# Attention and two mixture layers on one core: the first mixture layer's work behind the attention, 256 or 512 tokens at a time

## The chip, the core and the metric

The kernel runs on one core of a Trainium2 chip. The core has TensorE (PE, matrix products into the banks of PSUM), VectorE (DVE), ScalarE (ACT), GpSimd (POOL) and SyncE (SP, whose queue issues all transfers here); each takes its own instructions strictly in order and waits on semaphores for the others. The metric is the device time of one execution in microseconds, the median of several runs.

## What is computed

Causal attention with a cumulative decay over 4 x 8 heads of 576 tokens and 64 dimensions, and then two feed-forward ("mixture") layers over 2304 tokens of 512 numbers. Cut to what matters:

```python
x = attention(q, k, v, f)                  # (2304, 512)
h = x @ w_in                               # (2304, 2048)
r = np.maximum(h, 0.0)
g = s * (r * r) + b
x = g @ w_out                              # (2304, 512): first mixture layer
h = x @ w2_in                              # (2304, 1024): second mixture layer
solu = h * softmax(h)
out = layernorm(solu, g_ln) @ w2_out       # (2304, 512)
```

## The kernel before, in words

Every product is made of parts. An operand is split into hi (rounded to the type fp32r) and lo (what is left), and a product is the sum of hi x hi, hi x lo and lo x hi, three products on PE.

**Order of the work.** The function declares pieces (`add`, line 72) with the names of what they read and write, an estimated duration and a priority. `Plan.run` (line 96) plays them through by these estimates: PE takes the ready piece with the lowest priority number, every other engine the one with the lowest sum of ready time and priority. The instructions are issued in that order, so each engine's queue, SP's too, is fixed when the kernel is built. Transfers with a negative priority go at once; others wait in the plan while more than 3 us of transfers are outstanding.

**Stages.** Attention comes first (some 316 us). The first mixture layer has two passes, because its weights don't all fit beside the attention: the first pass applies three of the eight slices of 256 hidden units (`first`) to all tokens and stores the sum to `x2p_d`; the second applies the other five (`rest`) and adds that sum. Then comes the second layer, 18 tiles of 128 tokens (`tile2`, line 883).

**One chunk of the first layer** (`job`, line 787) is 256 tokens. `x_load` (line 760) fetches x in two summands from `xs_d` (one into `xraw`, one into `xlo`), adds them, and splits the sum into `xhi` and `xlo`; both passes do this. For each slice there are 24 products of h (lines 807 to 818, 128 x 128 weights against 256 columns), the gate (relu on ACT, line 822; the square, line 823; gh, line 844 to 846; gl, line 833), and 24 products of x2 (lines 852 to 864). PE's priority is 4 per slice for h and 4 per slice + 9 for x2, so that h of the next two slices comes ahead of x2 of a slice, and 100 per chunk:

```python
add("PE", 6 * mm(CH), h_mm, ..., 1000 + 100 * n + 4 * m)
add("PE", 6 * mm(CH), x_mm, ..., 1000 + 100 * n + 4 * m + 9)
```

Then x2 is emptied into `x2o` and stored (first pass by ACT, line 871; second pass by DVE with `x2p`, line 868).

**What is there twice.** The first four chunks (`NB`) run among the attention's pieces with one bank for h and two for x2. When the attention is over, `extend` (line 1017) opens tiles in its place: a second pair `xhi1`, `xlo1`, a second x2 of two banks and three more banks for h. From chunk 4 on, jobs alternate between the two pairs of x buffers (`j = n % 2`) and of x2, and rotate over four banks of h. Chunk 4 itself uses the old pair and the old x2, which don't depend on `extend` (the name `"ext"`). r is there twice, gh and gl three times.

**Beside this stage** the second pass's weights and the second layer's are loaded and unpacked from 64-bit floats (`load_w`, line 696: transfer, ACT line 713, DVE lines 715, 717 and 720, then hi and lo), from the end of the attention on.

Of the kernel before, what the change touches and what calls it, by code (L numbers as in the profile page):

```python
# [20 lines left out]
FS = (3, 3, 3, 3, 3, 3, 3, 3, 3)  # L21
# [39 lines left out]
class Plan:  # L61
    """Orders the work of all engines: of the pieces whose inputs are there by an estimate, each engine takes the first.

    Pieces are declared in an order that is right; which of them have to wait for which follows from the names of what
    they read and write. The instructions are then issued in the order in which the pieces start by the estimate."""
# [6 lines left out]
    def add(self, eng, dur, fn, r=(), w=(), pri=0, bytes=None, after=(), until=None):  # L72
        """An engine's piece of dur ns, or by engine a choice of (dur, fn); bytes for a transfer; lower pri first."""
# [22 lines left out]
    def run(self):  # L96
# [87 lines left out]
def mm(n):  # L184
    return 2 + n / 2.4
# [3 lines left out]
def kernel(  # L189
# [38 lines left out]
    x2_d = dram.tile([KD, 128, NT], F32, name="x2_d")  # L228

# [12 lines left out]
    ident = const.tile([128, 128], F32, name="ident")  # L242
    mask = const.tile([128, 512], F32, name="mask")
    maskt = const.tile([128, 288], F32, name="maskt")
# [16 lines left out]
    xhis, xlos = ([moe.tile([128, KD, CH], F32R, name=x)] for x in ("xhi", "xlo"))  # L261
# [3 lines left out]
    QW = S + 64  # L265
    raw = tiles(att, [128, 2, S], F32, "raw", 2)
# [22 lines left out]
    # The first batch's first blocks have the mixture layer's banks as well.  # L289
# [62 lines left out]
    # Two pairs side by side. Their scores come by products of their parts, and their decay by products with rows of ones.  # L352
# [17 lines left out]
    # The tensor engine's clock rises after some microseconds of work on all rows: products of zeros until the first ones.  # L370
# [44 lines left out]
    def early_split(g):  # L415
        """The parts of two pairs' queries and keys."""
# [9 lines left out]
    # The odd heads' queries have their last rows first.  # L426
# [4 lines left out]
    def take(keys):  # L431
        """The tiles of these names pass from one use to the next."""
# [5 lines left out]
    # Both heads' first two blocks of queries, one head's third and fourth, both heads' tails, the other head's third  # L438
    # and fourth. The first batch's first blocks come first, for the mixture layer to start with them.
# [60 lines left out]
    def unit(s, p, i):  # L500
# [3 lines left out]
        if part:  # L504
# [5 lines left out]
            def scores(x, c, kc):  # L510
                """The products that make 128 queries' scores."""
# [100 lines left out]
        if tl:  # L612
            # The last 64 keys of the tails; lo goes below hi.
# [146 lines left out]
    def x_load(n, c, src, hi, lo, khi, klo, b=BX, x=[]):  # L760
        """Loads tokens and splits them; from the attention they come in two parts."""
# [5 lines left out]
        for g in range(2 if first else 1):  # L767
# [5 lines left out]
            if src is xs_d:  # L773
# [4 lines left out]
                add("SP", 650, lambda lo_=lo_, view=view: nc.sync.dma_start(out=f32(lo_()), in_=view[1]), rk + x, kl,  # L778
                    min(b, BS), bytes=512 * sz)
                P.first = P.first or len(P.ops) - 1  # L780
                tt(lambda raw_=raw_: raw_, lambda raw_=raw_: raw_, lambda lo_=lo_: f32(lo_()), sz, ALU.add, kl, kx, b)
            else:
                dma(raw_, src[ks, :, cs].rearrange("k p t -> p k t"), [("x2d", c)], kx, 512 * sz, b)
            copy(hi_, lambda raw_=raw_: raw_, sz, kx + x, kh, b)
            tt(lo_, lambda raw_=raw_: raw_, lambda hi_=hi_: f32(hi_()), sz, ALU.subtract, kx + kh, kl, b)

    def job(n, c, fps, last, b=BMOE):
        ext = n >= NB
        j = n % 2 if ext else 0
        khi, klo = (("xx", 2), ("xx", 3)) if j == 0 else (("xhi1",), ("xlo1",))  # L790
        hi, lo = (lambda: xhis[j]), (lambda: xlos[j])
        x_load(n, c, xs_d, hi, lo, khi, klo, x=["ext"] if j else [])
        nh = 4 if ext else 1
        jx2 = n % 2 if ext else 0
        kx2 = ("x2", jx2)
        x2 = lambda: x2ps[jx2]
        if last:
            dma_late(lambda: late["x2p"], x2p_d[:, :, c * CH:(c + 1) * CH].rearrange("k p t -> p k t"),
                     [("x2pd", c)], ["x2p"], 524288)
        for m, fp in enumerate(fps):  # L800
            ta, tb, ka, kb = weights[fp]
            jh = slot("h4", 4) if ext else 0
            kh = ("h", jh)
            h = lambda jh=jh: hps[jh]
            for g in range(2):
                for u in range(2):
                    def h_mm(u=u, g=g, h=h, ta=ta):
                        wh, wl = ta[0], ta[1]
                        for kc in (2 * g, 2 * g + 1):
                            o = kc * 256 + u * 128  # L810
                            a_, b_ = wh[:, o:o + 128], wl[:, o:o + 128]
                            t = h()[:, u, :]
                            for x, (w_, v_) in enumerate(((a_, hi()), (a_, lo()), (b_, hi()))):
                                nc.tensor.matmul(t, w_, v_[:, kc, :], start=kc == 0 and u == 0 and x == 0,  # L814
                                                 stop=kc == KD - 1 and x == 2, skip_group_check=True)

                    add("PE", 6 * mm(CH), h_mm, [khi + (g,), klo + (g,)] + wkeys(ka) + (["ext"] if jh else []), [kh],
                        1000 + 100 * n + 4 * m)
            jr, jg = slot("r", 2), slot("g", 3)
            r, gh, gl = rs_[jr], ghs[jg], gls[jg]  # L820
            kr, kgh, kgl = ("r", jr), ("gh", jg), ("gl", jg)
            add("ACT", act_p(512), lambda h=h, r=r: nc.scalar.activation(out=r, in_=h(), func=AF.Relu), [kh], [kr], b)  # L822
            def square(eng, r=r):
                if eng == "DVE":
                    nc.vector.scalar_tensor_tensor(out=r, in0=r, scalar=s_sb, in1=r, op0=ALU.mult, op1=ALU.mult)
# [287 lines left out]
```

## Time and profile before

| what | value |
|---|---|
| median of 3 runs | 901.32 us |
| lowest and highest | 900.86 and 901.57 us |
| span of the profiled execution | 902.3 us |
| own time of that execution | its span; none besides it is recorded |
| PE busy | 840.7 us, 93% |
| DVE, ACT, POOL busy | 538.8, 445.5, 355.7 us |
| products on PE | 5749, with as many weight loads |

The span is the time between the first and the last instruction of one execution, on the only core. Times in rows count from the span's start. A line number is that of the kernel before; L316 to L325 are helpers that copy, or add and subtract two tensors. "gl<-r,b_sb,gh" reads: gl is written from r, b_sb and gh. PE's products are pipelined, so the length of a single one (some 280 ns) is more than the distance to the next one's start. A wait's "releaser" is the instruction that ended it.

### The profile page before, as it was taken

What the parts mean: (1) busy time and instruction counts of PE and PEld (TensorE: products, weight loads), DVE (VectorE), ACT (ScalarE), POOL (GpSimd) and SP (SyncE); (2) the same over time, 40 slices, a digit from 0 to 9 for tenths busy, and PEclk for the clock granted to TensorE, in tenths of its full rate; (3) what the DMA queues carried; (4) which work ended last, traced back from release to release, by engine and by line L of the source; (5) the groups of instructions that cost most, each with busy time, mean ns of one, the idle gap of its engine ahead of it and who ended that gap; (6) DMA issues with size and microseconds to landing.
All of it is one profiled execution on the core that took longest, in us unless ns stands there. A gap on an engine that the chain in (4) does not pass through costs nothing.

```text
span 902.3 us, 15528 instructions
## 1 busy us (share of the span) xinstructions
PE 840.7 (93%) x5749; PEld 782.7 (87%) x5749; DVE 538.8 (60%) x1122; ACT 445.5 (49%) x981; POOL 355.7 (39%) x398
## 2 busy tenths in 40 slices
PE   7868889889899999898989999999999999999998
PEld 7747778888899999797989999999998888888886
DVE  8888897768678747877988321222213544444451
ACT  4666678758688646554355324332332333333342
POOL 6768786645645355545634111111113401111000
PEclk7689799999899999999999999999999999999999
DMA  6689999799896275664455312232112111100001
GB/s 197 163 206 235 247 258 248 183 251 226 201 232 189 86 271 176 194 198 135 141 187 187 95 45 73 71 94 86 32 47 71 48 46 48 46 24 12 24 36 46
DMA packets 84413, 120.82 MB, mean 134 GB/s; under 512 B 7010, under 2 KB 62818, under 8 KB 84338
## 3 DMA queue, kind: packets, MB, share of 16 engines
q1 hardware_dynamic: 84338, 119.84, 48.0%
q8 instruction: 45, 0.74, 0.3%
q14 instruction: 30, 0.25, 0.1%
HBM read 70.12 MB, written 23.89 MB: 104 GB/s over the span
## 4 chain that ended last, share of the span: by engine, by line
PE 60%; DMA 14%; DVE 12%; issue 5%; ACT 4%; POOL 3%; SPq 2%; ACTq 0%; POOLq 0%; DVEq 0%
PE h L814 13%; PE ph L916 10%; PE x L860 5%; PE x L861 5%; PE x L858 5%; PE po L960 4%; PE po L959 4%; PE po L961 4%; DMA k<-raw 3%; PE S L549 2%; DVE wr L717 2%; PE PT L601 2%; DVE wr L720 2%; PE O L670 2%; DMA k<-Hh 2%
## 5 line engine op out<-in xcount | busy, mean ns | idle before, releaser
L835 DVE SCALAR_TENSOR_TENSOR gl<-r,b_sb,gh 128x512 fp32r<-128x512 f32 x65 | 55.9, 860 | 134.3 <-POOL gh L846 132.9
L814 PE MATMUL h<-xhi,u 128*128 128x256 f32 x720 | 134.0, 283 | 0.0
L846 POOL TENSOR_SCALAR gh<-r,b_sb 128x512 fp32r<-128x512 f32 x57 | 46.3, 812 | 197.0 <-ACT r L828 169.1
L586 POOL TENSOR_SCALAR e<-e,m 128x128 f32<-128x128 f32 (+4 forms) x144 | 101.0, 713 | 53.7 <-DVE m L582 32.8
L814 PEld LDWEIGHTS h<-xhi,u 128*128 128x128 f32 x720 | 114.3, 192 | 0.0
L822 ACT ACTIVATE r<-h 128x512 f32<-128x512 f32 x72 | 42.8, 594 | 131.2 <-PE h L814 127.7
L858 PE MATMUL x<-gh,u 128*128 128x256 f32 x360 | 103.3, 287 | 3.9 <-POOL gh L846 3.9
L860 PE MATMUL x<-gl,u 128*128 128x256 f32 x360 | 103.9, 288 | 1.6 <-DVE gl L835 1.4
L861 PE MATMUL x<-gh,u 128*128 128x256 f32 x360 | 103.2, 287 | 0.0
L814 PE MATMUL h<-xlo,u 128*128 128x256 f32 x360 | 102.0, 283 | 0.0
L573 ACT ACTIVATE e<-e,m 128x128 f32<-128x128 f32 (+4 forms) x144 | 84.0, 586 | 19.8 <-DVE m L536 19.3
L814 PE MATMUL h<-xhi,w 128*128 128x256 f32 x432 | 86.5, 287 | 2.0 <-POOL xhi L316 2.0
L601 PE MATMUL PT<-ident,e 128*128 128x128 f32 x384 | 65.1, 296 | 15.3 <-DVE pbl L609 8.5
L549 PE MATMUL S<-k,q 68*128 68x384 f32 (+2 forms) x248 | 65.5, 375 | 9.8 <-DMA k<-raw 3.4
L858 PEld LDWEIGHTS x<-gh,u 128*128 128x128 f32 x360 | 70.5, 196 | 4.3 <-POOL gh L846 4.3
L814 PEld LDWEIGHTS h<-xhi,w 128*128 128x128 f32 x432 | 71.1, 193 | 2.8 <-POOL xhi L316 2.3
L536 DVE CUSTOM_DVE_ANT_0 e<-S,mask 128x512 f32<-128x512 f32 (+4 forms) x136 | 63.1, 486 | 16.6 <-PE S L549 13.8
L860 PEld LDWEIGHTS x<-gl,u 128*128 128x128 f32 x360 | 70.4, 196 | 2.4 <-DVE gl L835 2.4
L860 PE MATMUL x<-gl,w 128*128 128x256 f32 x216 | 63.8, 295 | 7.7 <-DVE gl L835 5.2
L861 PEld LDWEIGHTS x<-gh,u 128*128 128x128 f32 x360 | 70.6, 196 | 0.0
L814 PEld LDWEIGHTS h<-xlo,u 128*128 128x128 f32 x360 | 69.2, 192 | 0.0
L916 PE MATMUL ph<-w,xh 128*128 128x512 f32 x256 | 68.7, 390 | 0.0
(214 smaller groups left out, 2224.3 us busy)
## 6 DMA issues: line engine op xcount, KB each, us to landing
xraw<-xs_d SPq DMA_DIRECT2D x17, 512.0 KB, 4.5
xlo<-xs_d SPq DMA_DIRECT2D x17, 512.0 KB, 4.7
q<-Hh SPq DMA_DIRECT2D x28, 288.0 KB, 5.8
k<-Hh SPq DMA_DIRECT2D x28, 288.0 KB, 7.7
wraw<-in_moe_w_in_dram SPq DMA_DIRECT2D x14, 512.0 KB, 3.8
wraw<-in_moe_w_out_dram SPq DMA_DIRECT2D x14, 512.0 KB, 4.5
xs_d<-xt SPq DMA_DIRECT2D x16, 320.0 KB, 4.3
raw<-in_moe_w_in_dram SPq DMA_DIRECT2D x10, 512.0 KB
```

The source lines that it names most:

```text
L536: nc.vector.tensor_tensor_reduce(out=e_, in0=sp, in1=mk, scale=-scale, scalar=init, op0=ALU.add, op1=ALU.min, accum_out=acc)
L549: nc.tensor.matmul(o, a, b, start=i == 0, stop=i == len(mms) - 1)
L573: nc.scalar.activation(out=e[:, c], in_=e[:, c], func=AF.Exp, scale=-1.0, bias=m[:, j:j + 1], accum_out=m[:, 2 + j:3 + j])
L586: nc.gpsimd.tensor_scalar(out=e[:, c], in0=e[:, c], scalar1=m[:, 4 + j:5 + j], scalar2=1.0, op0=ALU.mult, op1=ALU.mult)
L601: nc.tensor.transpose(pt[:, kb, :], e[:, 128 * kb:128 * kb + 128], ident)
L814: nc.tensor.matmul(t, w_, v_[:, kc, :], start=kc == 0 and u == 0 and x == 0, stop=kc == KD - 1 and x == 2, skip_group_check=True)
L835: nc.vector.scalar_tensor_tensor(out=gl, in0=r, scalar=b_sb, in1=f32(gh), op0=ALU.add, op1=ALU.subtract)
L846: "POOL": (662, lambda r=r, gh=gh: nc.gpsimd.tensor_scalar(out=gh, in0=r, scalar1=1.0, scalar2=b_sb, op0=ALU.mult, op1=ALU.add))}, 0, 0, [ ...
L858: nc.tensor.matmul(t, a_, gh[:, u, :], start=st and u == 0 and d % 2 == 0, stop=False, skip_group_check=True)
L860: nc.tensor.matmul(t, a_, gl[:, u, :], start=False, stop=False, skip_group_check=True)
L861: nc.tensor.matmul(t, b_, gh[:, u, :], start=False, stop=fin and u == 1, skip_group_check=True)
L916: nc.tensor.matmul(h()[:, n:n + 512], st_, mv[:, n:n + 512], start=kc == 0 and mv is wh and st_ is a, stop=kc == KD - 1 and st_ is b)
```

## The change

Chunks 0 to 3, under the attention, stay as they are (`job`), with one store more: the summed x goes to a new array `xc_d`. From there on `job_wide` takes 512 tokens at a time: tokens 1024 to 2047 in two jobs and the last 256 in a job of 256 for the first pass, 0 to 2047 in four jobs and the last 256 in one for the second. An item of work is one half (128) of a slice's hidden units for 512 tokens, so a wide job has six items in the first pass and ten in the second, each of 12 products of h and 12 of x2 with 512 columns. The x of a job is in one buffer: raw x takes all of `xr2` (xraw and x2o of before), hi the new `xh`, lo both old tiles; the second pass reads the sum from `xc_d`. Four banks hold x2 of 512 tokens, four others rotate for h. x2 is emptied block by block through two tiles `xo`, and `xp` (two tiles of 512) takes x2p, or x's second summand in the first pass. The gate is moved into a function `gate` without a change to it, the masks move to the attention's pool, and comments are dropped. The core of the diff:

```diff
-        xhis.append(pool.tile([128, KD, CH], F32R, name="xhi1"))
-        xlos.append(pool.tile([128, KD, CH], F32R, name="xlo1"))
-        late["x2p"] = pool.tile([128, KD, CH], F32, name="x2p")
+        late["xh"] = pool.tile([128, 2, KD, CH], F32R, name="xh")
+        for x in ("xo", "xp"):
+            late[x] = pool.tile([128, 2, 512], F32, name=x)
...
-        x2ps.append(ps.tile([128, KD, CH], F32, name="x22"))
-        hps.extend(tiles(ps, [128, 2, CH], F32, "h4", 3))
+        late["x2w"] = tiles(ps, [128, 512], F32, "x2w", KD)
+        late["h"] = ps.tile([128, 512], F32, name="h1")
...
-    jobs = [(c, first[:FS[c]], None) for c in range(NCH)] + [(c, first[FS[c]:] + rest, True) for c in range(NCH)]
+    jobs = [(c * CH, CH, first, False) for c in range(NB)]
+    jobs += [(t, w, first, False) for t, w in spans(NB * CH)] + [(t, w, rest, True) for t, w in spans(0)]
...
+                dma(xc_d[ks, :, cs].rearrange("k p t -> p k t"), raw_, kx, [("xc", c, k) for k in range(ks.start, ks.stop)],
+                    512 * sz)
...
+    def job_x(n, t0, width, fps, last):
...
+        for g in range(2):
+            ks = slice(2 * g, 2 * g + 2)
...
+            if last:
+                dma(raw_[:, ks], xc_d[ks, :, cs].rearrange("k p t -> p k t"), xk, rk, size, BX)
+            else:
...
+                dma(raw_[:, ks], view[0], sk, rk, size, BX)
+                second_ = lambda: late["xp"].rearrange("p u n -> p (u n)")[:, 0:2 * width].rearrange("p (k n) -> p k n", k=2)
+                dma_late(second_, view[1], sk, [("xp", 0), ("xp", 1)], size, BX)
+                tt(lambda ks=ks: raw_[:, ks], lambda ks=ks: raw_[:, ks], second_, 2 * width, ALU.add,
+                   [("xp", 0), ("xp", 1)], rk, BX)
+                dma(xc_d[ks, :, cs].rearrange("k p t -> p k t"), raw_[:, ks], rk, xk, size)
+            step = 1 if x else 2
+            for k in range(2 * g, 2 * g + 2, step):
+                a = slice(k, k + step)
+                copy(lambda a=a: hi()[:, a], lambda a=a: raw_[:, a], 512, [kr(k), "ext"], [khi(k)], BX)
+                tt(lambda a=a: lo()[:, a], lambda a=a: raw_[:, a], lambda a=a: f32(hi()[:, a]), 512, ALU.subtract,
+                   [kr(k), khi(k), "ext"], [klo(k)], BX)
...
+    def job_wide(n, t0, width, fps, last, b=BMOE):
...
+        hbanks = [(lambda: flat(hps[0]), ("h", 0)), (lambda: late["h"], ("h", 1))]
+        if x:
+            hbanks += [(lambda g=g: flat(x2ps[0][:, 2 * g:2 * g + 2]), ("x2", 0, g)) for g in range(2)]
+        work = [(m, fp, us) for m, fp in enumerate(fps) for us in ([(0,), (1,)] if x else [(0, 1)])]
+        for j, (m, fp, us) in enumerate(work):
+            ta, tb, ka, kb = weights[fp]
+            h, kh = hbanks[slot("hb" if x else "hb2", len(hbanks))]
...
+                    add("PE", 6 * mm(width), lambda h=h, u=u, g=g, ta=ta, us=us: h_mms(part(h(), u), ta, hi(), lo(), g, u, u == us[0]),
+                        [k(kc) for k in (khi, klo) for kc in (2 * g, 2 * g + 1)] + wkeys(ka) + ["ext"], [kh], base + 4 * j)
+            gh, gl, kgh, kgl = gate(lambda h=h: h().rearrange("p (u n) -> p u n", u=2), kh, slot("r", 2), slot("g", 3), b)
...
+                    add("PE", 6 * mm(width), x_mm, [kgh, kgl] + wkeys(kb) + ["ext"],
+                        [("x2w", 2 * g), ("x2w", 2 * g + 1)] if x else [("x2w", g)], base + 4 * j + 9)
...
+        for d in range(KD if x else 2):
...
+            if last:
+                dma_late(lambda tile_=tile_: tile_("xp"), shape(x2p_d), keys("x2pd"), [("xp", d % 2)], 262144)
+                add("DVE", dve(512), lambda d=d: nc.vector.tensor_add(
+                    out=late["xo"][:, d % 2], in0=late["x2w"][d], in1=late["xp"][:, d % 2]),
+                    [("x2w", d), ("xp", d % 2)], [("xo", d % 2)], b)
+            else:
+                add("ACT", act_p(512), lambda d=d: nc.scalar.copy(out=late["xo"][:, d % 2], in_=late["x2w"][d]),
+                    [("x2w", d)], [("xo", d % 2)], b)
```

## Rows read from the trace of the kernel before

**Rows 1.** The page: span and the engines' busy time.
```profile
span 902.3 us, 15528 instructions
...
PE 840.7 (93%) x5749; PEld 782.7 (87%) x5749; DVE 538.8 (60%) x1122; ACT 445.5 (49%) x981; POOL 355.7 (39%) x398
```

**Rows 2.** Busy time by stretches, PE: us, busy (products), granted clock, DMA share, GB/s.
```profile
100.00:200.00 100.00, 86.33 (x592) 0.90 0.99 236
317.80:689.00 371.20, 357.80 (x2907) 0.99 0.38 123
500.00:669.00 169.00, 169.00 (x1411) 1.00 0.24 73
```

**Rows 3.** Chain of waits, 495 to 905 us: start, length, what.
```profile
511.07 8.64 PE h L814 x72
...
792.59 10.88 PE ph L916 x48
```

**Rows 4.** PE's waits, 317 to 500 us: us in total, times, longest.
```profile
PE x L860 <- DVE gl L835: 6.3, 7, 1.7
PE x L858 <- POOL gh L846: 3.9, 2, 2.3
PE x L860 <- POOL gl L838: 2.4, 2, 1.5
PE x L858 <- ACT gh L844: 0.6, 1, 0.6
```

**Rows 5.** Timeline of PE: start, length, line, tiles, shape, count.
```profile
315.63 0.21 PE L670 MATMUL O<-pbh,vs 128*128 128x64 f32 x1
...
318.15 0.40 PE L814 MATMUL h<-xhi,w 128*128 128x256 f32 x2
...
427.15 0.41 PE L861 MATMUL x<-gh,u 128*128 128x256 f32 x1
...
429.71 0.37 PE L861 MATMUL x<-gh,u 128*128 128x256 f32 x1
...
460.79 0.41 PE L861 MATMUL x<-gh,u 128*128 128x256 f32 x1
...
463.78 0.40 PE L860 MATMUL x<-gl,u 128*128 128x256 f32 x1
```

**Rows 6.** Timeline of SP's queue of transfers, 316 to 323 us.
```profile
316.39 0.36 SPq L311 DMA_DIRECT2D xs_d<-xt  x1
319.21 0.36 SPq L311 DMA_DIRECT2D x2p_d<-xraw  x1
319.80 0.36 SPq L778 DMA_DIRECT2D xlo<-xs_d  x1
...
322.35 1.38 SPq L707 DMA_DIRECT2D wraw<-in_moe_w_in_dram  x2
```

**Rows 7.** Transfers by line: count, KB each, median us to landing.
```profile
xlo<-xs_d SPq DMA_DIRECT2D x17, 512.0 KB, 4.7
```

**Rows 8.** Timeline of DVE, 324 to 329 us: add and split of x.
```profile
324.81 1.23 DVE L324 TENSOR_TENSOR xraw<-xraw,xlo 128x1024 f32<-128x1024 f32 x1 [0.22 <-DVE gl L835]
...
327.39 1.22 DVE L324 TENSOR_TENSOR xlo<-xraw,xhi 128x1024 fp32r<-128x1024 f32 x1
```

**Rows 9.** Groups by line, 500 to 660 us: busy, mean ns | idle, releaser.
```profile
L835 DVE SCALAR_TENSOR_TENSOR gl<-r,b_sb,gh 128x512 fp32r<-128x512 f32 x27 | 20.3, 751 | 94.1 <-POOL gh L846 94.1
L828 ACT ACTIVATE r<-r,s_sb 128x512 f32<-128x512 f32 x28 | 20.3, 724 | 0.9
L846 POOL TENSOR_SCALAR gh<-r,b_sb 128x512 fp32r<-128x512 f32 x27 | 18.8, 697 | 114.0 <-ACT r L828 100.0 <-issue 14.0
L827 ACT ACTIVATE r<-r 128x512 f32<-128x512 f32 x28 | 17.7, 631 | 0.9
L822 ACT ACTIVATE r<-h 128x512 f32<-128x512 f32 x27 | 16.1, 597 | 104.8 <-PE h L814 104.8
```

**Rows 10.** Waits of SP's queue, 317 to 500 us.
```profile
SPq L707 <- DVE wr L720: 96.8, 29, 9.7
```

More of the change, by code (lines that the diff above doesn't have):

```diff
@@ L20 @@
 FP1 = 3
-FS = (3, 3, 3, 3, 3, 3, 3, 3, 3)
 NB = 4
@@ L785, in x_load, with dma_late @@
+            copy(hi_, lambda raw_=raw_: raw_, sz, kx, kh, b)
             tt(lo_, lambda raw_=raw_: raw_, lambda hi_=hi_: f32(hi_()), sz, ALU.subtract, kx + kh, kl, b)
[L787 to L799, printed above, removed]
+    def dma_late(out, in_, r, w, size, pri=0):
+        add("SP", 650, lambda: nc.sync.dma_start(out=out(), in_=in_), r + ["ext"], w, pri, bytes=size)
@@ L800, in job @@
+    def job(n, c, fps, b=BMOE):
+        hi, lo, khi, klo = (lambda: xhis[0]), (lambda: xlos[0]), ("xx", 2), ("xx", 3)
+        x_load(n, c, xs_d, hi, lo, khi, klo)
+        kx2, x2, h, kh = ("x2", 0), (lambda: x2ps[0]), (lambda: hps[0]), ("h", 0)
         for m, fp in enumerate(fps):
             ta, tb, ka, kb = weights[fp]
-            jh = slot("h4", 4) if ext else 0
-            kh = ("h", jh)
-            h = lambda jh=jh: hps[jh]
             for g in range(2):
                 for u in range(2):
[L807 to L818, printed above, removed]
@@ L848, in job @@
-            add(ways(rest_, DVE=dve(512), POOL=pool2(512) + 662), 0, 0, [kgh], [kr, kgl], b)
+                    add("PE", 6 * mm(CH), lambda u=u, g=g, ta=ta: h_mms(h()[:, u, :], ta, hi(), lo(), g, u, u == 0),
+                        [khi + (g,), klo + (g,)] + wkeys(ka), [kh], 1000 + 100 * n + 4 * m)
+            gh, gl, kgh, kgl = gate(h, kh, slot("r", 2), slot("g", 3), b)
             st, fin = m == 0, m == len(fps) - 1
@@ L864, in job @@
-                    add("PE", 6 * mm(CH), x_mm, [kgh, kgl] + wkeys(kb) + (["ext"] if jx2 else []), [kx2 + (g,)], 1000 + 100 * n + 4 * m + 9)
+                            x_mms(x2()[:, d, :], tb, gh[:, u, :], gl[:, u, :], u, d, st and u == 0 and d % 2 == 0, fin and u == 1)
+                    add("PE", 6 * mm(CH), x_mm, [kgh, kgl] + wkeys(kb), [kx2 + (g,)], 1000 + 100 * n + 4 * m + 9)
         for g in range(2):
             a = slice(2 * g, 2 * g + 2)
+            add("ACT", act_p(512), lambda a=a: nc.scalar.copy(out=x2o[:, a], in_=x2()[:, a]), [kx2 + (g,)],
+                [("xx", 1, g)], b)
@@ new lines, in job, with h_mms @@
+        dma(x2p_d[:, :, c * CH:(c + 1) * CH].rearrange("k p t -> p k t"), x2o, [("xx", 1, 0), ("xx", 1, 1)],
+            [("x2pd", c, k) for k in range(KD)], 524288)
+    def h_mms(t, ta, hi, lo, g, u, first):
+        for kc in (2 * g, 2 * g + 1):
+            o = kc * 256 + u * 128
+            a_, b_ = ta[0][:, o:o + 128], ta[1][:, o:o + 128]
+            for x, (w_, v_) in enumerate(((a_, hi), (a_, lo), (b_, hi))):
+                nc.tensor.matmul(t, w_, v_[:, kc, :], start=kc == 0 and first and x == 0,
+                                 stop=kc == KD - 1 and x == 2, skip_group_check=True)
@@ L867, in job @@
             if last:
-                add("DVE", dve(512), lambda a=a: nc.vector.tensor_add(
-                    out=x2o[:, a], in0=x2()[:, a], in1=late["x2p"][:, a]), [kx2 + (g,), "x2p"], [("xx", 1, g)], b)
-            else:
-                add("ACT", act_p(512), lambda a=a: nc.scalar.copy(out=x2o[:, a], in_=x2()[:, a]), [kx2 + (g,)],
-                    [("xx", 1, g)], b)
-        dst = x2_d if last else x2p_d
-        dma(dst[:, :, c * CH:(c + 1) * CH].rearrange("k p t -> p k t"), x2o, [("xx", 1, 0), ("xx", 1, 1)],
-            [("x2d" if last else "x2pd", c)], 524288)
@@ L881 @@
+            to = shape(dst)
+            add("SP", 650, lambda to=to, tile_=tile_: nc.sync.dma_start(out=to, in_=tile_("xo")), [("xo", d % 2)],
+                keys("x2d" if last else "x2pd"), 0, bytes=262144)
     NTILE = NT // 128
@@ L1042 @@
     late_w = [(Lazy(), Lazy()) for _ in range(2 * len(rest))]
-    for n, (c, fps, last) in enumerate(jobs):
+    for n, (t0, width, fps, last) in enumerate(jobs):
         if n == NB:
-            add("NONE", 0, extend, (), ["ext"], after=range(natt))
-        if n == NCH:
+            ext = add("NONE", 0, extend, (), ["ext"], after=range(natt))
+        if last and not t0:
             for i, fp in enumerate(rest):
                 load_fp(fp, late_w[2 * i], late_w[2 * i + 1], (f"u{2 * i}",), (f"u{2 * i + 1}",), "wraw2", 0, after=[ext])
-        job(n, c, fps, last)
-        if n == NB:
-            ext = P.writer["ext"]
+        if n < NB:
+            job(n, t0 // CH, fps)
+        else:
+            job_wide(n, t0, width, fps, last)
     x_load(2 * NCH, 0, x2_d, lambda: xhis[0], lambda: xlos[0], ("xx", 2), ("xx", 3))
```

134 lines of the change are left out of this document (88 added, 46 removed).

## The prediction

> **What bounds the kernel now.** The page comes first: its engine lines and slices say that TensorE is busy for 93% of the span [rows 1]. That share is an average, so the second view is busy time by stretches: from the end of the attention to the last product of the first layer (317.8 to 689.0 us) PE is busy for 357.8 of 371.2 us, and from 500 to 669 us for all of 169.0 [rows 2]. The other engines can only show there as holes in PE's line. So the third view is the chain of waits, for PE's pace: 72 products of 256 columns take 8.64 us, 120.0 ns each, and 48 products of 512 columns, in the second layer, 10.88 us, 226.7 ns each [rows 3]. Twice 120.0 less 226.7 is 13.3 ns: what PE spends per product beyond its columns. This is what the change can win.
>
> The stage by that pace: five chunks of the first pass (3 slices of 256 hidden units, 48 products each) and nine of the second (5 slices) are 720 + 2160 = 2880 products at 120.0 ns, 345.6 us. With the 24 products of 512 columns of the second layer that run inside, 5.4 us, the work is 351.0 of 371.2 us, so 20.2 us are lost. The waits of PE show 13.2 us of these (6.3 + 3.9 + 2.4 + 0.6), each time products of x with the gate's outputs gh and gl [rows 4]. After the longer two, PE runs for a while at 1.2 GHz instead of 2.4: 13 products start 213 ns apart between 427.15 and 429.71 us and 15 between 460.79 and 463.78 [rows 5], 28 x 0.093 = 2.6 us. That makes 15.8 us, none of it after 500 us [rows 2]; by the times of the waits it falls on the five chunks of the first pass and the first two of the second, 2.3 us a chunk. The remaining 4.4 us I leave as they are.
>
> **The change, part by part.** *Pace.* Behind the attention the first pass has two jobs of 512 tokens and one of 256, the second four and one. A wide job has half the products: 144 in place of 288 in the first pass, 240 in place of 480 in the second; 2 x 144 + 4 x 240 = 1248 wide products, each in place of two. The gain is 1248 x 13.3 ns = 16.6 us. The bounds are 0 (a wide product costs two narrow ones) and these 16.6; I take the measured pace, since the wide products in rows 3 have the same types, 128 rows and one weight load each as those here will have.
> The Trainium skill, "TensorE: Matmul & The Clock Gate", section "Back-to-back issue gap", gives a gap of columns / 2.4 + 2.5 ns for a warm stream, by which a wide product would save only 2.5 ns against two narrow ones: an estimated gain of 3.1 us and a sum 13.5 us higher. The trace doesn't agree with it: its 120.0 and 226.7 ns lie 10.8 and 10.9 ns above that gap.
>
> *Start of the stage: x waits for the attention.* Now chunk 4 is fetched under the attention into buffers that exist there, and its first product starts at 318.15 us, with only chunk 3's last products between it and the attention's last one at 315.63 [rows 5]. Every wide job needs tiles that are opened behind the attention (xh, xp, xo, x2w). The first half of x (two of the four blocks of 128 rows) can come early into xraw, but its second summand goes to xp. The transfer that stands in that place now, into the second buffer of xlo, is issued at 319.80 us, right behind the store of x2p at 319.21 [rows 6]. Such a load lands 4.7 us later [rows 7]: 324.5. The add of 1024 columns takes 1.23 us, and the split into hi and lo of 1024 columns now ends 2.6 us after the add [rows 8]; cut into pieces of 512 on three engines I put it at 2.2. PE starts at 328.0: **9.9 us idle** (6.4 if the load is issued right behind the last store of the attention at 316.39; 13 if it waits for a late one). Such a hole is longer than those in rows 4, so I add one slow stretch, 1.3 us. The second half reuses xp: its load can be issued only after the add, at 325.8, with weight loads in front (the second pair of them at 322.35 [rows 6]); 4.7 and some 2 us for these put it at 332.5, and add and split at 335. Until then PE has four h banks of first halves, 4 x 6 x 226.7 ns = 5.4 us, slow stretch included until 334.7. I add 1.0 (0 to 4). Start: 9.9 + 1.3 + 1.0 = **12.2 us** (6.5 to 18).
>
> *Boundaries between jobs: one buffer.* hi and lo of the next job can be written only after the last h product of this one. Each engine that splits has gates queued behind it, and PE waits for both. The cover is what PE still has: with h two items ahead of x, the x pieces of three items, 3 x 12 x 226.7 ns = 8.2 us. Four copies and four subtractions of 512 columns, half of 1.22 us each for a subtraction [rows 8], spread over three engines need about 4 us: hidden, if raw x is there. The adds that now run for nine chunks of the second pass fall away (x is read back whole from xc); they are off the path already, so they give nothing.
>
> *Gate stalls.* A gate takes relu 0.60, two more ACT passes of 0.63 and 0.72, POOL 0.70 and DVE 0.75 us [rows 9], 3.4 us, longer when weights are in the queues. A job of three items gives each gate the cover of two pieces, 5.8 us. In a wide job of six or ten items that is so only for the first and the last; between them four pieces, 10.9 us. The stretch with the stalls holds four jobs (two wide, one of 256, the second pass's first) in place of seven chunks. At 2.3 us a job that is 9.0 us in place of 15.8 (bounds 4 and 15.8).
>
> *x2 in four banks, once.* The next job's first x piece waits until the four banks are emptied into two tiles xo, whose stores must land. The first two go at once, the others one store later, about 5 us. PE has 8.2 us of h first: nothing, and at most 2 us a boundary while SP's queue is held up. What this copy holds up on ACT is the next relu.
>
> *Under the attention.* Four chunks are stored to xc, 2.1 MB more on SP's queue and in the DMA engines, which between 100 and 200 us are already at 99% and 236 GB/s [rows 2]. The bounds are 0 and 8.9 us (2.1 MB at that rate, all on the path); PE hardly waits on transfers there, so I take 1.0. The larger number of smaller stores of x2 and x2p costs SP 0.4 us each, beside its idle time.
>
> **Sum.** -16.6 + 12.2 + (9.0 - 15.8) + 1.0 = -10.2 us against the profiled span of 902.3. No other time stands with that execution; it is 1.0 above the median of 901.32 (900.86 to 901.57). So 892.1 in the trace, **891.1** as a median. The loss in the stage stays about as it is; the pace is what is won.
>
> **Rivals.** (A) The start is shorter and the stalls go: load at 316.4, stalls 4. -16.6 + 8 + (4 - 15.8) = -20, **881**. For it speaks that in rows 2 nothing is lost once weights are done; against it the store of chunk 3's x2p, which must land before half of the x buffer is free.
> (B) Slower: x of the next wide job isn't in raw when the last h ends. xp serves both halves, so each job of the first pass takes two turns in SP's queue, one after the other, and there weight loads stand waiting for DVE: 96.8 us in 29 waits, 3.3 us each, the longest 9.7 [rows 10]. Price: 3.3 + 4.7 + 1.2 + 2.2 = 11 us for a half; exposed at the two next boundaries of the first pass, less their 2.3 us each, +17: **908**. It decides once x comes more than 8.2 us after the last h; a job leaves 33 us for both halves, which speaks against it.
> The Trainium skill, "Trainium Kernel Development and Optimization", section "Best Practices", asks for double buffers so that transfers lie beside work; this change takes one away. By that rule (B) would be the likeliest; no row of this trace shows a chunk that waits for x after 318 us, with two buffers.
> (C) The wide product costs almost what two narrow ones do, since in the second layer neighbouring products share their stationary operand more often: 891.1 + 13.3 = 904.4 with a fifth of the 16.6 us left, 907.7 with none. The rule of the gap above, by the Trainium skill's page "TensorE: Matmul & The Clock Gate", would put it at an estimated 904.6; rows 3 speak against it.
> (D) Bounds meet in the middle (start 18, stalls as before): -16.6 + 18 + 1 = +2.4 to -1: **about 902**, no change.
>
> **How the numbers follow.** What a measurement of this kernel tells from no change is 0.2%, 1.8 us. The forecast, with 884 to 899 around it, gets 0.58; (A) 0.15; (B) 0.13; (C) 0.05; (D) 0.09. So faster 0.73, same 0.09, slower 0.18. The range is 880 (A, with all low bounds) to 903 (start 18, stalls unchanged, attention 2); what is left out is most of (B) and (C).
>
> **What would show it.** In the profile of the changed kernel: wide products 227 ns apart (240 would be C); PE idle for about 10 us between 318 and 328 us, ended by a split of x that goes back to the load into xp; a run at 1.2 GHz behind it; waits of PE for gh and gl of less than 10 us in all; 500 to 660 us without a hole at the boundaries. Waits of h products for splits after 340 us would be (B). The forecast is wrong if PE starts before 322 us, if boundaries show holes of over 3 us, or if the attention ends more than 3 us later.

## Result and profile of the changed kernel

The changed kernel takes 910.64 us (median of 4 runs, 908.68 to 915.74), the kernel before 901.09 (4 runs, 900.41 to 901.57): a ratio of 1.0127, interval 1.0091 to 1.0164. It is slower by 9.6 us; the prediction said 891.1, faster, and its range ended at 903. The profiled execution took 910.68 us with a span of 908.8, 6.5 longer than the span of before.

The page: PE's busy share falls by one point against [rows 1], with 1248 products fewer.

```profile
span 908.8 us, 13126 instructions
...
PE 832.4 (92%) x4501; PEld 719.3 (79%) x4501; DVE 539.1 (59%) x1118; ACT 443.6 (49%) x977; POOL 390.4 (43%) x431
```

Busy time of PE by stretches, columns as in [rows 2]. Counted alike in both, from the start of chunk 3's last product to the start of the stage's last one, the stage takes 378.3 us in place of 369.9, 8.4 longer, so the loss lies inside it. It doesn't lie at its end: from 520 us on PE is busy throughout. It lies in the first 24 us (13 busy) and between 340 and 510.

```profile
316.00:694.50 378.50, 347.95 (x1654) 0.96 0.36 117
520.00:690.00 170.00, 169.31 (x842) 1.00 0.17 53
316.00:340.00 24.00, 13.05 (x44) 0.72 0.85 286
340.00:420.00 80.00, 71.62 (x329) 0.94 0.62 204
420.00:510.00 90.00, 79.47 (x363) 0.96 0.42 135
```

The same two later stretches before:

```profile
340.00:420.00 80.00, 73.55 (x598) 1.00 0.58 185
420.00:510.00 90.00, 84.58 (x671) 0.96 0.45 147
```

Busy time hides the slow clock, so I also added up, over PE's timeline, what lies between one start and the next beyond 120 ns (256 columns) or 227 ns (512). This holds idle time and slow clock alike (us lost, by the time of the profile, one profile each; the rows below the first two are the experiments told further down):

```
                           300-340  340-420  420-470  470-510  510-700
before                         3.2      8.5      9.4      0.3      0.1
after                         16.1     14.2      3.6     11.6      0.9
e1  chunk 4 narrow             8.9     15.3      3.8     10.0      0.9
e2  weights late              15.7     10.1      2.1      0.9      9.7
e5  more cover                16.3      9.9      8.6      5.4      1.8
e6  weights spread            15.4     13.1      0.8      1.0      0.9
e10 both                       7.5     14.5      0.8      1.0      1.1
e11 and last slices later      6.8      7.5      0.8      0.1      1.6
e3  before, weights late       3.1      9.2      1.4     -0.1      2.5
e12 before, weights spread     3.0     12.8      0.0      0.9      2.0
```

After less before is +12.9 at the start, +11.2 between 340 and 510 us and +0.8 behind; less the pace's 16.6 that is +8.3. Chunk 3's last product starts 1.6 us earlier in this profile (316.15 against 317.79), and the stage's last one 6.8 later (694.5 against 687.7): the sum closes. The first column carries over better from one execution to the next than the second: up to 500 us, e2 and e6 give every engine the same instructions in the same order, and so do e3 and e12, and still the stretch from 340 to 420 us differs by 3.0 and 3.6 us within these pairs. So the 5.7 us that it grows by from before to after is not far beyond this scatter.

**The pace** came as measured before. Timeline of PE in the second pass: wide products start 0.22 to 0.23 us apart.

```profile
507.06 0.39 PE L909 MATMUL x2w<-gh,u 128*128 128x512 f32 x1
507.29 0.39 PE L910 MATMUL x2w<-gl,u 128*128 128x512 f32 x1
```

**The start.** PE's timeline around the end of the attention, with the idle time before each in brackets: chunk 3's last product, then the first wide one, 9.24 us idle.

```profile
316.15 0.28 PE L911 MATMUL x<-gh,w 128*128 128x256 f32 x1
...
325.67 0.80 PE L903 MATMUL h<-xh,w 128*128 128x512 f32 x1 [9.24 <-DMA raw<-in_moe_w_in_dram]
...
327.47 0.80 PE L903 MATMUL h<-xhl,w 128*128 128x512 f32 x1 [1.00 <-POOL xhl L326]
```

The releaser named is a weight transfer that has nothing to do with this; the pieces of xh are what comes last. The timelines of SP, DVE and ACT show their chain: the second summand of x goes to xp at 318.27 us, behind the store of x2p; the add waits for it until 323.69; the first piece of xh, on ACT, ends 0.1 us before PE starts; the second half's load waits for the add.

```profile
317.56 0.36 SPq L312 DMA_DIRECT2D x2p_d<-xraw  x1
318.27 0.36 SPq L791 DMA_DIRECT2D xp<-xs_d  x1
...
324.94 0.37 SPq L791 DMA_DIRECT2D xp<-xs_d  x1
```

```profile
323.69 1.23 DVE L325 TENSOR_TENSOR xraw<-xraw,xp 128x1024 f32<-128x1024 f32 x1 [12.63 <-DMA xp<-xs_d]
...
325.60 0.69 DVE L325 TENSOR_TENSOR xhl<-xraw,xh 128x512 fp32r<-128x512 f32 x1 [0.68 <-ACT xh L315]
```

```profile
324.95 0.62 ACT L315 CAST xh<-xraw 128x512 fp32r<-128x512 f32 x1 [7.41 <-DVE xraw L325]
```

**The waits between 316 and 510 us** (us in total, times, longest; for before see [rows 4]). Without the first line, the start, products of x2w wait for gates for 16.6 us (5.6 + 5.4 + 3.9 + 1.7), up to 3.0 at a time; before, 13.2, up to 2.3. The line "x L903 <- ACT r" is new: two of the four h banks are halves of the old x2, and when the second of them is filled right behind the first, PE stops until the relu of the first has read it. That happens three times here and four times up to the stage's end, 3.2 us in all; the row at 375.55 is one of them.

```profile
PE h L903 <- DMA raw<-in_moe_w_in_dram: 9.2, 1, 9.2
PE x2w L909 <- POOL gh L865: 5.6, 3, 3.0
PE x2w L910 <- POOL gl L857: 5.4, 3, 2.5
PE x2w L910 <- DVE gl L854: 3.9, 4, 1.6
PE x L903 <- ACT r L840: 2.5, 3, 1.0
PE x2w L909 <- ACT gh L863: 1.7, 1, 1.7
PE h L903 <- POOL xhl L326: 1.2, 2, 1.0
```

```profile
375.55 0.50 PE L903 MATMUL x<-xh,w 128*128 128x512 f32 x1 [0.69 <-ACT r L840]
```

The largest waits for gates, at the end of the second pass's first wide job. PE's timeline: four holes, 7.3 us together; from 489.6 to 496.4 us the granted clock is at 1.2 GHz.

```profile
481.33 0.50 PE L909 MATMUL x2w<-gh,u 128*128 128x512 f32 x1 [0.69 <-POOL gh L865]
...
482.88 0.50 PE L910 MATMUL x2w<-gl,u 128*128 128x512 f32 x1 [1.05 <-DVE gl L854]
...
488.70 0.50 PE L909 MATMUL x2w<-gh,u 128*128 128x512 f32 x1 [3.03 <-POOL gh L865]
...
491.71 0.80 PE L910 MATMUL x2w<-gl,u 128*128 128x512 f32 x1 [2.51 <-POOL gl L857]
```

The last h product of the job ended at 477.9 us. ACT's timeline shows why its gate is late: between the relu of the item before (478.84) and its own (485.19) stand pieces of a second-layer weight, one waiting 1.46 us for its transfer and one 1.93 for DVE, and a split of the next job's x (the CAST), which with one buffer comes just here; POOL, too, works at splits from 481.25 to 485.76 us.

```profile
478.84 0.58 ACT L840 ACTIVATE r<-h 128x512 f32<-128x512 f32 x1
...
481.44 0.68 ACT L714 ACTIVATE wr<-wraw 128x512 f32<-128x512 f32 x1 [1.46 <-DMA wraw<-in_moe_w_out_dram]
482.02 0.60 ACT L315 CAST xh<-xraw 128x512 fp32r<-128x512 f32 x1
...
484.56 0.73 ACT L733 ACTIVATE v<-wr,gl_sb 128x512 fp32r<-128x512 f32 x1 [1.93 <-DVE wr L721]
485.19 0.58 ACT L840 ACTIVATE r<-h 128x512 f32<-128x512 f32 x1
```

The three gate operations on POOL that follow end at 491.65, 13.7 us after the h products; in a quiet stretch it is 3.7 (500 to 660 us). So two parts of the stage were open to test: the first job behind the attention, and what the second layer's weights do to the gates.

### The profile page after: what moved, and what is told of

Same layout as the page of the kernel before. It is cut to its first block, busy times and chain, and to the rows that moved or that the text cites. A ratio compares the mean times of both kernels' runs of the same rounds, so it can differ in the third digit from the quotient of the medians.

```text
span 908.8 us, 13126 instructions
## 1 busy us (share of the span) xinstructions
PE 832.4 (92%) x4501; PEld 719.3 (79%) x4501; DVE 539.1 (59%) x1118; ACT 443.6 (49%) x977; POOL 390.4 (43%) x431
## 4 chain that ended last, share of the span: by engine, by line
PE 62%; DVE 12%; DMA 12%; POOL 4%; issue 4%; ACT 3%; SPq 2%; POOLq 0%; ACTq 0%; DVEq 0%
PE ph L999 10%; PE h L903 9%; PE x L903 5%; PE x2w L910 4%; PE x2w L911 4%; PE x2w L909 4%; PE po L1042 4%; PE po L1044 4%; PE po L1043 4%; PE S L550 3%; PE O L671 3%; DVE wr L718 3%; PE PT L602 2%; DMA q<-raw 2%; DVE wr L721 2%
## 5 line engine op out<-in xcount | busy, mean ns | idle before, releaser
L910 PE MATMUL x2w<-gl,u 128*128 128x512 f32 (+1 forms) x200 | 74.9, 375 | 3.6 <-POOL gl L857 2.5
L909 PE MATMUL x2w<-gh,u 128*128 128x512 f32 (+1 forms) x200 | 74.5, 373 | 3.7 <-POOL gh L865 3.7
L911 PE MATMUL x2w<-gh,u 128*128 128x512 f32 (+1 forms) x200 | 74.4, 372 | 0.0
L602 PE MATMUL PT<-ident,e 128*128 128x128 f32 x384 | 64.2, 295 | 10.9 <-DVE pal L610 4.4
L537 DVE CUSTOM_DVE_ANT_0 e<-S,mask 128x512 f32<-128x512 f32 (+4 forms) x136 | 62.4, 487 | 16.2 <-PE S L550 12.4
L903 PE MATMUL h<-xh,u 128*128 128x512 f32 (+1 forms) x280 | 67.3, 344 | 0.0
L602 PEld LDWEIGHTS PT<-ident,e 128*128 128x128 f32 x384 | 46.1, 150 | 17.4 <-issue 7.7
L903 PE MATMUL h<-xhl,w 128*128 128x256 f32 (+1 forms) x312 | 54.5, 304 | 4.8 <-POOL xhl L317 2.7
L999 PEld LDWEIGHTS ph<-w,xh 128*128 128x128 f32 x256 | 47.9, 188 | 10.0
L903 PE MATMUL x<-xh,u 128*128 128x512 f32 x160 | 52.9, 391 | 2.5 <-ACT r L840 2.5
L610 DVE TENSOR_TENSOR pbl<-PT,pbh 128x512 fp32r<-128x512 f32 (+1 forms) x80 | 49.1, 628 | 5.6 <-ACT pbh L321 5.0
L550 PEld LDWEIGHTS S<-k,q 68*128 68x128 f32 (+1 forms) x248 | 41.1, 212 | 13.7 <-DVE m L537 6.7
L903 PEld LDWEIGHTS h<-xhl,w 128*128 128x128 f32 x312 | 44.3, 196 | 8.8 <-POOL xhl L317 2.9
```

The lines of the kernel that those rows point to most:

```text
L537: nc.vector.tensor_tensor_reduce(out=e_, in0=sp, in1=mk, scale=-scale, scalar=init, op0=ALU.add, op1=ALU.min, accum_out=acc)
L550: nc.tensor.matmul(o, a, b, start=i == 0, stop=i == len(mms) - 1)
L602: nc.tensor.transpose(pt[:, kb, :], e[:, 128 * kb:128 * kb + 128], ident)
L610: add("DVE", dve(n), lambda: nc.vector.tensor_tensor(out=lo, in0=src, in1=f32(hi), op=ALU.subtract), [kp, kh], [kl], ba)
L903: nc.tensor.matmul(t, w_, v_[:, kc, :], start=kc == 0 and first and x == 0, stop=kc == KD - 1 and x == 2, skip_group_check=True)
L909: nc.tensor.matmul(t, a_, gh, start=start, stop=False, skip_group_check=True)
```

## Experiments

Ratios are to runs of the kernel before on the same chip (medians 900.82 for e1 to e4, 899.79 for e5 to e8, 900.19 for e9 to e12).

**e1: chunk 4 stays in the 256 form**, so that its x comes under the attention; its x2 is emptied into xo, since the older buffer is gone by then.

```
-NB = 4
+NB = 5
...
+        ends = n == NB - 1
+        to = (lambda: late["xo"]...) if ends else (lambda: x2o)
```

> The changed kernel, but the first chunk behind the attention is taken in the old way, 256 tokens in buffers that are there under the attention; its x2 is emptied into xo so that both halves of the next job's x can be fetched meanwhile, and the 512-token jobs of the first pass start at token 1280. Theory S (the start): the 9.2 us hole ahead of the first wide product and the slow clock behind it come from x waiting for tiles opened at the attention's end. Then the hole goes, and the time falls by 8 to 12 us against the changed kernel's 910.6, to 899 to 903. Rival: something that ends with the attention itself (its last stores) holds PE whatever the job's width; then a hole of 6 us or more remains ahead of the second job behind the attention, and the time stays over 906.

901.89 us (10 runs), ratio 1.0025 (1.0000 to 1.0051): 8.7 less than the changed kernel, as theory S expected. PE's timeline has no hole any more where it was, and the longest one left up to 340 us is 2.1 us, a wait for a gate:

```profile
317.35 0.28 PE L915 MATMUL x<-gh,w 128*128 128x256 f32 x1
317.46 0.76 PE L907 MATMUL h<-xhl,w 128*128 128x256 f32 x5
```

Waiting for tiles that are opened at the attention's end is shown to cost some 9 us. The stalls behind it stay (table).

**e2: the second layer's weights are read only after the second pass's first wide job.** Here and in e3, `marks[n]` is the last piece of job n, counted from 0; the line that fills `marks` is left out.

```
...
-               after=[ext])
+               after=[marks[7]])
```

> The changed kernel, but the second layer's weights are fetched and unpacked only once the first wide job of the second pass has stored its result (about 500 us), not from the attention's end on. Theory Q (queues): the stalls between 340 and 505 us (some 29 us beyond the products' pace) are gates that stand in the in-order queues of ACT, DVE and POOL behind the unpacking of weights; those between 430 and 505 stand behind the second layer's. Then the 12 us lost between 470 and 505 shrink to under 3, and the time falls by 9 to 14 us, to 897 to 902. Rival B (one buffer): PE stalls there because it has no product of the next job while hi and lo wait for this job's last h; then most of these 12 us remain, and the time stays within 4 us of 910.6.

905.28 us (6 runs), ratio 1.0062 (1.0028 to 1.0097): 5.4 less than the changed kernel, about half of what was expected. By stretches, the hole at 470 to 510 us is gone, and a new one stands where the same work meets the next boundary:

```profile
420.00:510.00 90.00, 87.65 (x408) 1.00 0.26 80
510.00:660.00 150.00, 143.31 (x635) 0.98 0.27 88
```

```profile
538.98 0.50 PE L909 MATMUL x2w<-gh,u 128*128 128x512 f32 x1 [3.09 <-ACT gh L863]
...
541.97 0.79 PE L910 MATMUL x2w<-gl,u 128*128 128x512 f32 x1 [2.48 <-POOL gl L857]
```

The stall follows the weights to the next boundary that they meet (9.7 us lost behind 510 us): it isn't a property of one job.

**e3: the same move in the kernel before.**

```
...
-               after=[ext])
+               after=[marks[10]])
```

> The kernel before, with the same delay of the second layer's weights (until chunk 1 of the second pass is stored, about 480 us). Theory Q: the kernel before loses some 9 us between 420 and 470 us to the same queues; it gets 6 to 9 us faster, 892 to 895. Rival B: with two buffers for x the kernel before has nothing to lose there; within 2 us of 901.

894.53 us (9 runs), ratio 0.9951 (0.9913 to 0.9988): 6.3 less than the kernel before on the same chip. PE is busy for 89.1 of 90 us where it was for 84.6, and some 2 us come back later (table):

```profile
420.00:510.00 90.00, 89.09 (x740) 1.00 0.36 115
510.00:660.00 150.00, 148.43 (x1233) 1.00 0.30 97
```

So before, too, a large part of the stalls in [rows 4] was this unpacking.

**e4: the kernel before with one pair of x buffers.**

```
-        j = n % 2 if ext else 0
+        j = 0
```

> The kernel before, with one buffer for hi and lo of x in all its chunks (256 tokens, otherwise unchanged). Rival B: 14 boundaries between chunks behind the attention each lose 1 to 2 us, since the next chunk's h products can't fill the wait for the gates: 915 to 930. Theory Q: a boundary costs only where weights are unpacked (6 of the 14) and there under 1.5 us; none after 505 us: 901 to 910.

903.20 us (10 runs), ratio 1.0038 (1.0004 to 1.0073): 2.4 us more. Rival B is out for this form. Its waits of PE show what one buffer looks like, products of h that wait for splits, 8.4 us:

```profile
PE h L814 <- DVE xlo L324: 4.2, 4, 1.5
PE h L814 <- POOL xhi L316: 2.1, 4, 0.7
PE h L814 <- POOL xlo L325: 2.1, 1, 2.1
```

Such lines are missing from the changed kernel behind its start.

**e5: the x pieces of an item stand one item later** in the order, for more cover.

```
-  base + 4 * j + 9)
+  base + 4 * j + 13)
```

> The changed kernel, but PE's order lets the h products of three items, not two, go ahead of an item's x products (priority 4 per item + 13 instead of + 9). Nothing else changes. If the late gates are only uncovered at the ends of the wide jobs (cover of the last gate 5.4 us now, 8.2 us then), the holes at the ends of jobs shrink by 2.7 us each, at four ends up to 500 us: 5 to 10 us faster than 910.6, slow clock included. If the stalls come from splits of x standing in the queues, the holes stay: within 3 us.

909.73 us (4 runs), ratio 1.0122 (1.0101 to 1.0143): no gain in time, against 5 to 10 us expected. The holes move: 5.4 us lost at 470 to 510 in place of 11.6, but 8.6 at 420 to 470 in place of 3.6, and 9.9 at 340 to 420 in place of 14.2. Over the three stretches that is 23.9 in place of 29.4, so this profile does show 5.5 us less, but its attention ends 3.7 us later, and one profile can't settle either. What it does show is that one more item of cover leaves most of the stalls: the gates come late by more than one item's h.

**e6: the second layer's weights spread**: its eight weights in groups of three, three and two, each begun at the end of one of the second pass's first three jobs. `marks` holds the last pieces of these jobs.

```
...
-               after=[ext])
+               after=[marks[i // 3]])
```

> The changed kernel, but the second layer's weights are fetched in three groups, each begun when a wide job of the second pass has stored its result, so that a group is unpacked within a job and none at a boundary. Theory Q: an unpacking that meets a boundary costs some 10 us in the wide form (11.6 at 470 to 510 us in the changed kernel, 9.8 at 540 when it was moved there); without the meeting both losses go: under 3 us lost from 430 us on, time 894 to 900. Rival: the boundary costs by itself; then 5 us or more stay lost behind 430 us, time over 903.

898.24 us (10 runs), ratio 0.9988 (0.9959 to 1.0018): 12.4 less than the changed kernel and 7.0 less than e2, which begins as late but in one lump. From 420 to 470 us a gate now ends 3.6 us after its h products, where it was 8.3.

```profile
420.00:510.00 90.00, 88.75 (x411) 1.00 0.26 82
510.00:670.00 160.00, 159.31 (x781) 1.00 0.29 93
```

With e2 this is the clearest result: the same instructions, placed in smaller groups, are hidden.

**e7 and e8: one or two pairs of x buffers in the wide form.** Both leave out the last slice of hidden units of the second pass, whose room the second pair needs, and are compared with each other only.

```
-    rest = list(range(FP1, NFP))
+    rest = list(range(FP1, NFP - 1))
```

and in e8 the odd jobs use the pair xa, xb.

> The changed kernel without the last slice of 256 hidden units in the second pass (that part of the first layer is left out, for room in memory), as the measure for the next run. Four wide jobs less 48 products of 227 ns and one narrow job less 48 of 120 ns, 49 us of work: 858 to 865 us.

> The run before, the last slice left out too, with two buffers of hi and lo for the jobs behind the attention, used in turn. Rival B (one buffer): PE fills the wait for the last gates with the next job's h products; 8 us or more faster than the run with one buffer. Theory Q: the gates are as late and the next job's first x waits in their place; 0 to 5 us faster.

853.18 us (4 runs) with one pair, 862.75 (4 runs) with two: the second pair makes it 9.6 us slower. Neither theory had that. The first was itself expected at 858 to 865: not only the 49 us of work went, but stalls as well. That weakens the pair of runs as a test, for e7 loses only 5.2 us from 420 to 510 us (2.2 of them behind 470) where the changed kernel lost 15.2 (11.6). Stretches of e7, then of e8:

```profile
340.00:420.00 80.00, 72.10 (x338) 0.94 0.57 188
420.00:510.00 90.00, 85.40 (x394) 1.00 0.37 120
```

```profile
340.00:420.00 80.00, 70.41 (x298) 0.94 0.61 193
420.00:510.00 90.00, 81.22 (x388) 0.94 0.42 141
```

The loss lies among the stalled gates again. Why a second pair makes more of them is open; the planner puts the whole stage in another order with it. A second pair is no remedy by itself; whether it would have taken away the changed kernel's own stall at 470 to 510 us isn't shown, since e7 hardly has it.

**e9: e6 with every job 256 wide**, to measure the pace in the new form.

```
-        return [(t, min(512, NT - t)) for t in range(t0, NT, 512)]
+        return [(t, CH) for t in range(t0, NT, CH)]
```

> The changed kernel with the second layer's weights in three groups as in the run that was named for it, and all jobs behind the attention of 256 tokens in place of 512: one buffer of x, two banks of h, one pair of banks of x2, chunk by chunk. Against that run (898.2 us) it gives back the pace: 1248 x 13.3 ns = 16.6 us, and the boundaries of 14 jobs in place of 8. Theory P (the pace is won in full): 915 us or more. Rival (wide products win nothing on the path, since gates set the pace): within 5 us of 898.

917.11 us (4 runs), ratio 1.0163 (1.0105 to 1.0221), 18.9 more than e6. (Behind the attention's last product, the two profiles differ by 17.2 us; the attention itself ends 5.9 later in e9's.) Its chain has the pace of [rows 3]:

```profile
522.57 8.64 PE h L903 x72
```

**e10: e1 and e6 together.**

> The changed kernel with both repairs: the first chunk behind the attention in the old way with its x2 emptied into xo, and the second layer's weights in three groups. If the two losses are separate, the gains add: 910.6 - 8.7 - 12.4 = 889.5, range 886 to 893. If they share stalls, 893 to 898.

891.01 us (4 runs), ratio 0.9887 (0.9843 to 0.9932). The two gains add: 910.6 - 8.7 - 12.4 = 889.5 was expected.

**e11: e10, and the weights of the last two slices are read when the first pass is over.** `mark6` is the last piece of the first pass.

```
...
-  after=[ext])
+  after=[ext] if i < 3 else [mark6])
```

> As the run before, and of the second pass's own weights the last two slices are fetched only when the first pass is over. Theory Q: the stalls between 340 and 420 us (13 to 15 us lost) come from unpacking at the boundaries of the wide jobs there; one of the two boundaries is then free of it, so 4 to 8 us go: 882 to 889. Rival: those slices then come too late for the first job of the second pass; holes for weights appear behind 440 us, and the time is that of the run before or more.

881.89 us (4 runs, 879.92 to 888.34), ratio 0.9798 (0.9740 to 0.9855): the best of all, 18 us below the kernel before, and 9.1 below e10. 7.0 of these lie at 340 to 420 us, where the first pass met the unpacking of the second pass's weights (70.86 us busy in e10):

```profile
340.00:420.00 80.00, 74.70 (x321) 0.98 0.49 161
420.00:510.00 90.00, 89.31 (x394) 1.00 0.34 108
```

**e12: the kernel before with its weights spread as in e6.**

> The kernel before with the second layer's weights in three groups, begun when chunks 1, 3 and 5 of the second pass are stored. It had 894.5 us with all of them begun behind chunk 1. Groups meet boundaries of 256-token chunks wherever they lie, so little changes: 892 to 895.

896.33 us (10 runs), ratio 0.9950 (0.9921 to 0.9979), a little above what was expected. It is e10's counterpart in the 256 form, and e10 is 5.3 us below it: what the wide form is worth in all when neither the start's hole nor these weights stand in its way. In the two profiles the stage behind the attention is 11.7 us shorter in e10, and its attention ends 6.3 us later; whether that is more than scatter is open (see below). e11's move was not tried in the 256 form.

## Why the prediction was wrong

**Pace (-16.6): right.** 227 ns a wide product, and e9 against e6 gives 18.9 us for the whole form. Rival (C), that a wide product costs nearly two narrow ones, is out. The Trainium skill, "TensorE: Matmul & The Clock Gate", section "Back-to-back issue gap", gives the gap behind the prediction's estimate of 3.1 us for an isolated product; for a stream of weight loads and products, which this kernel has, it gives about 131 ns at 512 columns. The trace agrees with neither: 226.7 ns.

**Start (+12.2): right**, +12.9 by the table. It happened by the steps given: 9.2 us of idle time ended by a split of x that goes back to the load into xp, then a run at 1.2 GHz until 332.6 us. That the sum is so near is in part luck: the idle time was put at 9.9, and the slow run costs more than the 1.3 it was given (the first twelve products take 6.7 us, 1.0 of it idle, where 2.7 is the full clock's time), while the second half of x was waited for 0.7 us, not 1.0. In the trace before, chunk 4 starts at 317.91 us, not at 318.15. e1 gives 8.7 us back.

**Under the attention (+1.0): open.** The last product before the wide form starts 1.6 us earlier in this profile. But one profile can't settle 1 us: the attention's last product starts at 311.2 to 318.7 us in the ten profiles with the stores to xc (315.3 on average), and at 311.5 to 315.6 in the four without them (312.9). That is 2.4 us later on average, not clear of the scatter.

**Gate stalls (9.0 in place of 15.8): this step failed.** "At 2.3 us a job that is 9.0 us" made the loss a toll for each boundary, and fewer boundaries a gain. Measured, 340 to 510 us lose 29.4 us in place of 18.2, and waits for gh and gl come to 16.6 us where the prediction's own sign asked for less than 10. Two things stood behind it in the text.

First, the gate was costed at "3.4 us, longer when weights are in the queues", with the durations of [rows 9], from a stretch in which there are no weights; the "longer" was never priced. In the trace of before, from 420 to 470 us, a gate ends 7.8 us after its h products, up to 11.5, and that could have been read; after, it is 8.3, up to 10.8, and 13.7 behind 470. The gates are hardly later than they were.

Second, the loss was put down to jobs when it belonged to the weights' unpacking: when that is moved, the loss between 420 and 510 us falls from 15.2 to 1.8 (e6) and in the kernel before from 9.7 to 1.3 (e3; 2.4 come back later), without a job more or less.

Why the wide form loses more to the same unpacking is read from the traces, and no run separates it. I counted the products that PE runs between a gate's last h product and its first x product, the gate's cover. Before, 18 of the 27 gates whose x products start between 340 and 510 us have 5.8 us, and all 11.9 us of waits for gates come from these; the others have 8.6 or 11.5. After, the ten gates in the middles of the wide jobs have 10.9 or more, as the prediction says, and none of them stops PE, though they come up to 10.8 us late. All 16.4 us of waits fall on the other 16, towards the ends of jobs, which have 5.4 to 8.2. So the cover that the change adds lies where it is more than enough, and the ends are left as short as before. Besides these 4.5 us, the 11.2 us hold the new wait for a relu (2.5) and, as an estimate by what is left, some 4 us of slow clock: TensorE is at 1.2 GHz for 17.1 us of this stretch where it was for 6.8.

**Boundary splits, one buffer (nothing): right.** Behind 340 us PE's waits show no h product that waits for a split; (B), slower by that way, did not happen though its time of 908 is near the measured one. That "slower" came true, as in (B), is no credit to it: the mechanism had no rival of its own. Splits do stand in the gates' queues at the boundaries (482.02 us above); in e6 they still do, and 1.0 us is lost there. The Trainium skill, "Trainium Kernel Development and Optimization", section "Best Practices", asks for double buffers: in the 256 form the second pair is worth 2.4 us (e4), in the wide form, a slice left out, it cost 9.6 (e8).

**Sum.** In place of -16.6 + 12.2 - 6.8 + 1.0 it is -16.6 + 12.9 + 11.2 + 0.8 and 1.6 less at the attention's end, +6.7; the spans differ by 6.5. The medians differ by 9.6: the execution profiled before has no time of its own and was, by its span, perhaps 3 us longer than the median (the other profiled ones show 1.7 to 2.5 us between time and span); that was not measured, but its attention is the latest of the four without the stores to xc. The prediction had put it at 1.0.

What is shown by runs: the start's cost (e1), the pace (e9), that the unpacking of weights makes the stalls behind 420 us (e2, e3, e6) and part of those before (e11), and that the start and the second layer's weights together are more than the loss (e10, 891.0). What is read from traces alone: that the ends of the wide jobs are where the stalls fall. What stays open: how much of the growth from 340 to 420 us is scatter, the 7.5 us that the first pass still loses there in e11, the attention's end, and e8.

## What to carry to other kernels

Latency that a chain of several engines may take is read from the stretch where the queues are full, not from the quiet one; larger tiles give the chains in their middle more cover, but the last ones of a tile have no more than before, and there cover that is just short stops the engine. Work for later stages (weights to be unpacked) belongs in small groups away from such boundaries: here the same instructions cost 12.4 us more in one lump, begun early, than spread. The first tile behind a phase change should use the buffers that exist before it.

## What was not expected of the hardware

A stall costs more than its idle time: behind the holes between 340 and 510 us the granted clock is at 1.2 GHz from 366.7 to 370.1, 404.3 to 411.1 and 489.6 to 496.4 us. In the last case PE is idle for 7.3 us, and 6.8 us at half speed cost up to 3.4 more.

A DVE pass over 512 columns of a weight (L718, L721) takes between 0.67 and 1.78 us in the same kernel, and in the trace the long ones go with work on POOL. Between 320 and 700 us there are 72 such passes: the 32 during which POOL does nothing take 0.67 to 0.69 us; the 26 that overlap a POOL operation on two tensors take 1.65 in the median, 25 of them over 0.9. The traces of before and e6 show the same. Minimum, median and maximum in ns of L721 between 440 and 493 us, and one long pass, on the way to the largest stall, with the POOL operation beside it:

```profile
L721 DVE SCALAR_TENSOR_TENSOR wr<-wraw,wr x13: 676/691/1774, 442.3 to 492.8; 128x512 uint32<-128x512 uint32 x13
```

```profile
482.75 1.77 DVE L721 SCALAR_TENSOR_TENSOR wr<-wraw,wr 128x512 uint32<-128x512 uint32 x1
482.37 1.60 POOL L326 TENSOR_TENSOR xhl<-xraw,xh 128x512 fp32r<-128x512 f32 x1
```

No run moved the POOL work away, so that it is the cause isn't shown. And the kernel before spreads from 895.97 to 907.25 us over 26 runs on one chip, more than the three runs shown at first (900.86 to 901.57) let one think.
